# Attention, two-layer MoE and soft MoE on one core: leaky ReLU of H as one parametric ReLU on ScalarE

## The chip, the cores and the metric

The kernel runs on one core of a Trainium2 chip. The metric is the device time of one execution in microseconds (us); the times of before are the median of three runs. The engines are named as the profile names them: PE (TensorE matmuls) and PEld (its weight loads), DVE (VectorE), ACT (ScalarE), POOL (GpSimd), SP (the queue from which the DMAs are issued). Each works through its own list of instructions in order, and waits for another engine by semaphore.

## What is computed

Causal attention over 4 batches of 12 heads (448 positions, head size 64), then a two-layer MLP with a leaky ReLU, then a soft mixture of experts (32 slots, 8 experts):

```python
h = x @ w_in                    # x: 1792 x 768 (attention output), w_in: 768 x 2048
g = np.maximum(0.01 * h, h)     # leaky ReLU: the part that is changed
x = g @ w_out                   # w_out: 2048 x 768
logits = x @ phi                # soft MoE: softmax over tokens and over slots,
...                             # slot inputs, two expert layers, combination
```

## The kernel before

Attention runs in 24 steps, one for each pair of heads (six pairs to a batch). A step writes maxima of the scores (S), scores (T), their exponentials (P, ACT line 397), denominators (dn, rs) and the output O; line 472 scales O to x16, the two halves of x in 16 bits, from which the MLP reads.

H, the product x @ w_in, is made in units: for batch b and column block f (16 blocks of 128 columns) 18 matmuls add up H of 128 x 448 in one bank of PSUM. `up(b)` issues these units. While batch b+1 is in attention, `stage` mixes the sixteen units of batch b into it, about one unit to each of the 18 slots of a batch; this is so for batches 0, 1 and 2. In that time H has a single buffer (`HB[0]` is 1), so the next unit's first matmul waits until the last unit's H has been read. Batch 3's units come after attention, with three buffers, mixed with the transposes of earlier batches' g and the softmax sums (`combine`). After that only the experts are left, whose weights w stream in from memory.

Of each H, ACT line 628 makes g = H * iv, with a scale per partition, and DVE line 629 then reads H again and makes g = max(H * 0.01 iv, g). The two scales lie in iv, made by ACT lines 596 and 597 (one pair of 1-column instructions to a unit in batch 0, one pair of 16 columns for each later batch). H is free when both have read it. g of batches 0 and 1 is stored to memory (g_far, line 631, SP), and fetched back later (gb); g of batches 2 and 3 goes to the logits (L, line 578) and the transposes (gps, line 565).

Beside this, weights are prepared: w_in comes in as raw 64-bit numbers (raw_i), which DVE lines 199 to 201, ACT lines 196, 197 and 215 and POOL lines 216 and 223 turn into two 16-bit halves (w16); DVE lines 113 to 121 make the scale w_s for that. w_out (raw_o, cv_o) goes the same way to the small product wprime (tiles wt, wp_ps, wf_ps). Each new v (line 311) is reduced by DVE line 324.

The order on each engine is set by a scheduler that works with its own estimate of time; attention and `up` carry a higher priority than the preparation, and the matmuls issued through `in_order` keep the order in which they are written.

Of the kernel before, what the change touches and what calls it, by code (L numbers as in the profile page):

```python
# [10 lines left out]
F32 = mybir.dt.float32  # L11
# [4 lines left out]
AF = mybir.ActivationFunctionType  # L16
ALU = mybir.AluOpType
# [5 lines left out]
SLOPE = 0.01  # L23
# [11 lines left out]
def tile_attn_moe_softmoe(ctx: ExitStack, tc: tile.TileContext, q, k, v, w_in, w_out, phi, w1, w2, out, dbg=None):  # L35
    nc = tc.nc
# [11 lines left out]
    NF = DFF // 128  # L48
# [4 lines left out]
    const = ctx.enter_context(tc.tile_pool(name="const", bufs=1))  # L53
# [70 lines left out]
    inv_v = [None] * B  # L124
    inv_w = const.tile([128, NF], F32, name="inv_w")
    iv = [None] * B
# [153 lines left out]
    def need(u):  # L280
        while u not in ready:
            if not running:
                prep_start()
            prep_step()
# [276 lines left out]
    def transpose_g(b, f):  # L561
        g = gts[b, f]
        ps = ps_tr(f"gps{b}_{f}", (CP, NI, 128))
        for i in range(NI):
            tr(ps[:, i], g[:, CP * i : CP * (i + 1)], ident)
        dst = g_nat[:, :, 128 * f : 128 * (f + 1)]
        if f % 2 == 0:
            nc.scalar.copy(dst, ps)  # L568
        else:
            nc.vector.tensor_copy(dst, ps)  # L570

    def logits(b, f4):

        ps = ps_tr(f"L{b}_{f4}", (128, S))
        for f in range(f4, f4 + 4):
            r = 32 * (f % 4)
            need(("o", f))
            mm(ps[r : r + 32, :], wprime[:, f], gts[b, f], start=True, stop=True, skip_group_check=True)
        if f4 == 0:
            l4s[b] = mainp.tile([128, S], F32, tag="l4", name=f"l4_{b}")  # L580
            nc.vector.tensor_copy(l4s[b], ps)
        else:
            nc.vector.tensor_tensor(l4s[b], ps, l4s[b], ALU.add)

    def up(b, before=()):
        before = list(before)
        queue = []
        group = 0
        far = b < 2
        if b == B - 1:  # L590
            spare = xpool.tile([128, CHUNK // 4], F32, tag="x16", name="g_spare")
        iv[b] = const.tile([128, 2, NF], F32, tag="iv", bufs=2, name=f"iv{b}")

        def scales(j):

            nc.scalar.activation(iv[b][:, 0, j], inv_w[:, j], AF.Copy, scale=inv_v[b])
            nc.scalar.activation(iv[b][:, 1, j], iv[b][:, 0, j], AF.Copy, scale=SLOPE)

        if b > 0:
            scales(slice(0, NF))  # L600
        for f in range(NF):
            if b == 0:
                need(("i", f))
                scales(slice(f, f + 1))
            wq, fo = w16[f // 4], 128 * (f % 4)
            ps = psum.tile([128, S], F32, tag="H", bufs=HB[0], name=f"H{b}_{f}")
            step = 0
            for c in range(NP):
                for wh, xh in ((0, 0), (1, 0), (0, 1)):
                    mm(ps, wq[:, wh, c, fo : fo + 128], x16[b][:, c, xh, :], start=step == 0, stop=step == 17)  # L610
                    step += 1
                if b == B - 1:
                    if before:
                        before.pop(0)()
                    elif queue and queue[0] < f - (c < 3):
                        transpose_g(b, queue.pop(0))
                elif b == B - 2 and c in (2, 4) and queue and queue[0] < f - 1:
                    transpose_g(b, queue.pop(0))
            if not far and not before and f >= group + 5:
                logits(b, group)  # L620
                group += 4
            if b == B - 1 and f < NSPARE:
                g = spare[:, S * f : S * (f + 1)]
            else:
                g = mainp.tile([128, S], F32, tag="g", bufs=GBUF if b > 1 else 3, name=f"g{b}_{f}")
            gts[b, f] = g
            queue.append(f)
            nc.scalar.activation(g, ps, AF.Copy, scale=iv[b][:, 0, f : f + 1])  # L628
            nc.vector.scalar_tensor_tensor(g, ps, iv[b][:, 1, f : f + 1], g, ALU.mult, ALU.max)  # L629
            if far:  # L630
                nc.sync.dma_start(g_far[b, f], g)
            yield
        if far:
            return
        while before:
            before.pop(0)()
        while queue or group < NF:
            if group < NF:
                logits(b, group)
                group += 4  # L640
            for _ in range(4):
                if queue:
                    transpose_g(b, queue.pop(0))
# [119 lines left out]
    if True:  # L763
# [15 lines left out]
        for b in range(1, 4):  # L779
            if b == 3:  # L780
                tc_release(pools[1])
                tc_release(mainp)
                mainp = tc.alloc_tile_pool(name="mainp", bufs=1, reuse_waits="tile")
                pools[2] = tc.alloc_tile_pool(name="conv", bufs=1, side="right", reuse_waits="tile")
                load_raw()
                g_nat = mainp.tile([CP, NI, DFF], F32, name="g_nat")
            stage(SLOTS * NP, sum(EARLY[: b + 1]) if b < 3 else 2 * NF, up(b - 1))
# [54 lines left out]
        for _ in up(B - 1, spread(combine(B - 2)) + late):  # L842
            pass
# [127 lines left out]
        for x, (t0, nt, c0, cols) in enumerate(pieces):  # L971
# [4 lines left out]
            for h in (0, 1) if cols == DM else (c0 // DH,):  # L976
                for t in range(nt):
                    g = (t0 + t) % 4
# [55 lines left out]
```

## Time and profile before

| | |
|---|---|
| median of three runs | 726.96 us (726.59 to 730.62) |
| the profiled execution's own time | 722.34 us |
| its span, first to last instruction | 720.6 us |
| granted clock of TensorE, mean | 0.958 |
| PE busy | 615.5 us (85%) |
| DVE busy | 378.6 us (53%) |
| ACT busy | 304.7 us (42%) |
| POOL busy | 232.1 us (32%) |

The profiled execution lies 4.6 us under the median of the runs, and 1.7 us of its time lie outside the span. A share of the span is an average over stages. The first unit of H starts at 117 us, attention ends at about 480 us, batch 3's last unit at 594 us, and the experts take the rest.

### The profile page before, as it was taken

Reading aid. Unit: us, or ns where it says so; the run is one execution under the profiler, and the core shown is the slowest. Engines: PE = TensorE matmul, PEld = TensorE weight load, DVE = VectorE, ACT = ScalarE, POOL = GpSimd, SP = SyncE. Lnnn points to the kernel's source line nnn. Section 1 sums busy time; section 2 is a strip of 40 time slices with the busy share of each in tenths; the row PEclk is TensorE's granted clock in tenths of the full one; section 3 lists DMA queues with packets and bytes.
Section 4 is the critical chain, followed back from the end, with each engine's and each line's share of the span. In section 5 each row is a group of like instructions: output and inputs, shape, how many; then the busy total and the mean of one; then the engine's idle time right before and its main releaser. Section 6 shows DMA issues by size and latency. Waiting matters only on the chain.

```text
span 720.6 us, 12298 instructions
## 1 busy us (share of the span) xinstructions
PE 615.5 (85%) x4764; PEld 348.7 (48%) x4764; DVE 378.6 (53%) x941; ACT 304.7 (42%) x615; POOL 232.1 (32%) x247
## 2 busy tenths in 40 slices
PE   3788749888898999899999999999999998984572
PEld 2455535544454555455555555544655543541131
DVE  5887655688985654665475565444445333010022
ACT  1777643667875456554355544422222220110022
POOL 4477733467856423452143343310000000000000
PEclk9999977999999999999999999999999999999787
DMA  9933263455355446421153221018758148999988
GB/s 196 258 84 78 46 190 113 109 165 152 101 165 186 133 122 206 139 92 59 50 148 96 95 62 41 21 52 306 276 200 331 64 178 317 408 400 399 393 287 258
DMA packets 117706, 125.67 MB, mean 174 GB/s; under 512 B 69520, under 2 KB 99216, under 8 KB 117648
## 3 DMA queue, kind: packets, MB, share of 16 engines
q1 hardware_dynamic: 117648, 124.90, 53.6%
q8 instruction: 37, 0.61, 0.4%
q14 instruction: 21, 0.17, 0.1%
HBM read 105.74 MB, written 19.14 MB: 173 GB/s over the span
## 4 chain that ended last, share of the span: by engine, by line
PE 51%; DMA 14%; DVE 14%; ACT 9%; POOL 4%; issue 4%; SPq 2%; DVEq 0%; ACTq 0%; POOLq 0%
PE H L100 22%; DMA w<-in_moe_w_dram 8%; PE O L100 6%; PE gps L100 4%; DVE rs L439 3%; DMA v<-in_v_dram 3%; DVE junk L361 2%; DMA raw_o<-in_moe_w_out_dram 2%; PE pg L100 2%; PE ph L899 2%; PE T L100 2%; PE L L100 2%; ACT mr L373 2%; DMA raw_i_None<-in_moe_w_in_dram 2%; ACT g L628 2%
## 5 line engine op out<-in xcount | busy, mean ns | idle before, releaser
L100 PE MATMUL H<-x,w 128*128 128x448 f16 x1152 | 240.9, 354 | 7.3 <-DVE g L629 6.1
L100 PEld LDWEIGHTS <-w 128*128 128x128 f16 x1152 | 109.2, 98 | 109.9 <-issue 27.7
L361 DVE CUSTOM_DVE_ANT_0 junk<-S,mask 112x448 bf16<-112x448 f32 (+1 forms) x192 | 84.6, 441 | 37.5 <-PE S L100 35.3
L629 DVE SCALAR_TENSOR_TENSOR g<-H,iv,g 128x448 f32<-128x448 f32 x58 | 39.5, 682 | 75.5 <-ACT g L628 75.5
L401 POOL TENSOR_SCALAR_AFFINE_SELECT P<-P 112x448 f32<-112x448 f32 x48 | 29.4, 612 | 141.6 <-ACT P L397 141.5
L397 ACT ACTIVATE P<-T 112x672 f32<-112x672 f32 (+1 forms) x72 | 56.8, 790 | 23.1 <-PE T L100 22.9
L628 ACT ACTIVATE g<-H,iv 128x448 f32<-128x448 f32 x58 | 36.6, 631 | 70.5 <-PE H L100 62.3
L100 PE MATMUL T<-qkt 64*112 64x336 f32 (+3 forms) x576 | 59.2, 317 | 6.1 <-ACT P L397 5.4
L100 PE MATMUL O<-P,v 112*64 112x448 f32 (+3 forms) x384 | 56.9, 439 | 6.4 <-POOL P L401 6.0
L439 DVE RECIPROCAL rs<-rs 128x224 f32<-128x224 f32 x36 | 53.3, 1522 | 1.6 <-ACT rs L437 1.6
L100 PEld LDWEIGHTS T<-qkt 64*112 64x112 f32 x576 | 44.6, 182 | 14.4 <-ACT P L397 6.6
L979 PE MATMUL po<-w,hz 128*32 128x384 f32 x256 | 29.0, 575 | 25.2 <-DMA w<-in_moe_w_dram 25.2
L410 POOL TENSOR_TENSOR tsum<-tsum,P 112x448 f32<-112x448 f32 (+1 forms) x48 | 45.9, 956 | 2.8
L100 PEld LDWEIGHTS O<-P,v 112*64 112x64 f32 x384 | 26.8, 146 | 36.1 <-issue 17.3
L373 ACT ACTIVATE mr<-mps,own 128x112 fp32r<-128x112 f32 x96 | 26.2, 357 | 42.8 <-PE mps L100 42.8
L568 ACT COPY g_nat<-gps 112x512 f32<-112x512 f32 x32 | 18.7, 586 | 55.3 <-PE gps L100 55.3
L406 POOL TENSOR_TENSOR tsum<-P 112x672 f32<-112x672 f32 x24 | 40.7, 1698 | 1.8
L570 DVE COPY g_nat<-gps 112x512 f32<-112x512 f32 x32 | 22.1, 689 | 36.1 <-PE gps L100 35.8
L100 PE MATMUL S<-qkt 64*112 64x448 f32 (+1 forms) x192 | 33.0, 384 | 7.4 <-DVE mxe L361 5.7
L892 POOL MEMSET hz<- 128x256 f32 x2 | 0.6, 312 | 116.2 <-PE pg L100 116.2
L216 POOL TENSOR_TENSOR cv_i_None<-cv_i_None,cs_i_None 128x768 f32<-128x768 f32 x16 | 26.8, 1683 | 30.0 <-ACT cs_i_None L215 29.8
L100 PE MATMUL T<-mr,onesr 64*112 64x448 f32 (+1 forms) x192 | 32.1, 331 | 3.5 <-ACT mr L373 3.5
(184 smaller groups left out, 935.0 us busy)
## 6 DMA issues: line engine op xcount, KB each, us to landing
w<-in_moe_w_dram SPq DMA_DIRECT2D x32, 1536.0 KB, 18.2
raw_i_None<-in_moe_w_in_dram SPq DMA_DIRECT2D x16, 768.0 KB, 5.6
raw_o_None<-in_moe_w_out_dram SPq DMA_DIRECT2D x10, 768.0 KB, 5.0
g_far<-g SPq DMA_DIRECT2D x32, 224.0 KB, 2.0
gb<-g_far SPq DMA_DIRECT2D x8, 896.0 KB, 7.6
wo<-wsc SPq DMA_DIRECT2D x4, 1536.0 KB, 7.0
qk<-in_q_dram SPq DMA_DIRECT2D x48, 112.0 KB, 2.5
qk<-in_k_dram SPq DMA_DIRECT2D x48, 112.0 KB, 2.8
```

The source lines that it names most:

```text
L100: op(*args, **kwargs)
L216: nc.gpsimd.tensor_tensor(t, t, sg, ALU.mult)
L361: nc.vector.tensor_tensor_reduce(out=junk[:, :w], in0=ps[:, a, at : at + w], in1=mask[:, S - w :], scale=-1.0, scalar=3e38, op0=ALU.add, o ...
L373: nc.scalar.activation(mr[:, i], ps, AF.Copy, scale=own[:, i : i + 1])
L397: nc.scalar.activation(x[:, :, o : o + at], ps[:, :, :at], AF.Exp, scale=SCALE)
L401: nc.gpsimd.affine_select(out=d, in_=d, compare_op=ALU.is_ge, fill=0.0, base=0, pattern=[[0, 4], [1, CP]], channel_multiplier=-1,)
L406: nc.gpsimd.tensor_tensor(tsum[:CP], p[0][:CP, :, 0, CP:], p[0][:CP, :, 1, : S - CP], ALU.add)
L410: nc.gpsimd.tensor_tensor(y, y, p[1][:CP, :, j, : S - CP * (j + 2)], ALU.add)
L439: nc.vector.reciprocal(rs[:, c : c + S // 2], rs[:, c : c + S // 2])
L628: nc.scalar.activation(g, ps, AF.Copy, scale=iv[b][:, 0, f : f + 1])
L629: nc.vector.scalar_tensor_tensor(g, ps, iv[b][:, 1, f : f + 1], g, ALU.mult, ALU.max)
L979: nc.tensor.matmul(po[h][32 * g : 32 * g + 32], hp[:, (t0 + t) % 8], wt[:, t, DH * h - c0 : DH * (h + 1) - c0], start=t0 + t < 4, stop=t0 ...
```

## The change

One instruction takes the place of two: ACT makes g with its parametric ReLU function, scale iv and slope 0.01, straight from H. DVE line 629 goes, 64 times. The second half of iv and ACT line 597 go, 19 times. Everything behind line 625 moves up by two lines: the new line is 627, and g_far is stored by line 629.

```diff
-        iv[b] = const.tile([128, 2, NF], F32, tag="iv", bufs=2, name=f"iv{b}")
+        iv[b] = const.tile([128, NF], F32, tag="iv", bufs=2, name=f"iv{b}")
 
         def scales(j):
 
-            nc.scalar.activation(iv[b][:, 0, j], inv_w[:, j], AF.Copy, scale=inv_v[b])
-            nc.scalar.activation(iv[b][:, 1, j], iv[b][:, 0, j], AF.Copy, scale=SLOPE)
+            nc.scalar.activation(iv[b][:, j], inv_w[:, j], AF.Copy, scale=inv_v[b])
...
-            nc.scalar.activation(g, ps, AF.Copy, scale=iv[b][:, 0, f : f + 1])
-            nc.vector.scalar_tensor_tensor(g, ps, iv[b][:, 1, f : f + 1], g, ALU.mult, ALU.max)
+            nc.scalar.activation(g, ps, AF.Prelu, scale=iv[b][:, f : f + 1], alpha=SLOPE)
             if far:
                 nc.sync.dma_start(g_far[b, f], g)
```

The scheduler lays out the whole program anew. PE's list stays as it was but for four small neighbouring swaps. DVE's loses its 64 rows, and some preparation moves by a few places.

On DVE, behind the first two attention outputs of batch 1 (junk is the pass over the maxima, rs the inverse denominators, cv_i raw w_in), before:

```order
L439 RECIPROCAL rs_1680<-rs_1680 128x224 x2
L199 TENSOR_REDUCE w_am_1837<-cv_i_None 128x1
L472 SCALAR_TENSOR_TENSOR rs_1680<-O_1603,v_s,rs_1680 128x448
L629 SCALAR_TENSOR_TENSOR g_4_1730<-H_4_1711,iv_1378,g_4_1730 128x448
L200 TENSOR_SCALAR cv_i_None<-cv_i_None 128x768
L361 ISA junk_1_0_1771,mxe_144<-S_1_1768,mask 112x224
```

and of the change:

```order
L439 RECIPROCAL rs_1672<-rs_1672 128x224 x2
L199 TENSOR_REDUCE w_am_1825<-cv_i_None 128x1
L472 SCALAR_TENSOR_TENSOR rs_1672<-O_1597,v_s,rs_1672 128x448
L200 TENSOR_SCALAR cv_i_None<-cv_i_None 128x768
L361 ISA junk_1_0_1761,mxe_144<-S_1_1758,mask 112x224
```

Only g_4 is gone; the rest stands in the same order.

On SP, at units 9 to 11 of batch 0, before:

```order
L302 DMA qk_2267<-in_q_dram 112x4x64 x2
L631 DMA g_far<-g_9_2203 128x448
L302 DMA qk_2267<-in_k_dram 112x4x64 x2
L173 DMA raw_o_None<-in_moe_w_out_dram 128x1536 x2
L311 DMA v_2516<-in_v_dram 112x8x64
L631 DMA g_far<-g_10_2296 128x448
L631 DMA g_far<-g_11_2364 128x448
```

and of the change:

```order
L629 DMA g_far<-g_9_2184 128x448
L302 DMA qk_2247<-in_q_dram 112x4x64 x2
L302 DMA qk_2247<-in_k_dram 112x4x64 x2
L173 DMA raw_o_None<-in_moe_w_out_dram 128x1536
L629 DMA g_far<-g_10_2275 128x448
L311 DMA v_2490<-in_v_dram 112x8x64
L173 DMA raw_o_None<-in_moe_w_out_dram 128x1536
L629 DMA g_far<-g_11_2341 128x448
```

The store of g_10 now stands ahead of the next load of v, and one load of raw_o behind it. The same happens to two more loads of v, at g_2 and g_13.

On ACT, the whole program of the change holds one table load, ahead of its first copy, as before:

```order
L1027 UNCONDITIONAL_BRANCH
L338 ACT_TABLE_LOAD
L338 CAST qkt_187<-qkps_0_188 128x448
L338 CAST qkt_187<-qkps_1_195 128x448
```

## Rows read from the trace of the kernel before

**Rows 1.** Busy time of each engine by stage (x instructions), granted clock, DMA share, GB/s

```profile
117.00:240.00 123.00, 110.54 (x759) 61.35 (x756) 94.19 (x237) 79.68 (x150) 74.40 (x59) 0.99 0.48 140
240.00:362.00 122.00, 116.07 (x895) 68.57 (x895) 69.53 (x155) 60.90 (x130) 44.06 (x41) 0.99 0.35 109
362.00:480.00 118.00, 111.48 (x833) 65.10 (x831) 62.67 (x142) 56.49 (x125) 41.01 (x45) 0.99 0.27 79
480.00:594.00 114.00, 112.34 (x754) 61.40 (x752) 51.26 (x102) 28.75 (x55) 1.03 (x1) 1.00 0.59 212
594.00:721.00 127.00, 82.86 (x835) 37.00 (x834) 21.14 (x64) 14.75 (x35) 2.62 (x16) 0.87 0.94 351
```

**Rows 2.** PE's waits, whole span: total us, times, longest

```profile
PE H L100 <- DVE g L629: 6.1, 6, 1.6
...
PE H L100 <- DVE w_s L118: 1.2, 1, 1.2
...
PE L L100 <- DVE g L629: 1.1, 2, 0.6
```

**Rows 3.** Groups by line, whole span: busy us, mean ns, idle before

```profile
L628 ACT ACTIVATE g<-H,iv 128x448 f32<-128x448 f32 x58 | 36.6, 631 | 70.5 <-PE H L100 62.3 <-PE L L100 6.6 <-DMA raw_o_None<-in_moe_w_out_dram 1.6
...
L629 DVE SCALAR_TENSOR_TENSOR g<-H,iv,g 128x448 f32<-128x448 f32 x58 | 39.5, 682 | 75.5 <-ACT g L628 75.5
...
L597 ACT ACTIVATE iv<-iv 128x1 f32<-128x1 f32 (+1 forms) x19 | 3.7, 201 | 0.2
...
L690 ACT ACTIVATE et<-lt,nm 128x448 f32<-128x448 f32 x4 | 2.5, 636 | 12.5 <-PE pl L100 12.5
...
L338 ACT ACT_TABLE_LOAD x1 | 1.3, 1283 | 0.8 <-PEq L1018 0.8
```

**Rows 4.** Timeline at three waits of H: start us, length us, engine and line

```profile
144.99 0.69 DVE L629 SCALAR_TENSOR_TENSOR g<-H,iv,g 128x448 f32<-128x448 f32 x1 [1.10 <-ACT g L628]
145.73 3.56 PE L100 MATMUL H<-x,w 128*128 128x448 f16 x18 [1.55 <-DVE g L629]
...
189.41 0.64 ACT L628 ACTIVATE g<-H,iv 128x448 f32<-128x448 f32 x1
191.57 0.67 DVE L629 SCALAR_TENSOR_TENSOR g<-H,iv,g 128x448 f32<-128x448 f32 x1
192.30 5.18 PE L100 MATMUL H<-x,w 128*128 128x448 f16 x18 [1.21 <-DVE w_s L118]
...
228.45 3.56 PE L100 MATMUL H<-x,w 128*128 128x448 f16 x18 [1.46 <-DVE g L629]
```

**Rows 5.** PE's waits for DVE's other work in 117:240, 240:362 and 362:480

```profile
PE S L100 <- DVE mxe L361: 2.3, 3, 1.1
...
PE w_ps L111 <- DVE qkt L339: 0.9, 1, 0.9
...
PE wf_ps L100 <- DVE qkt L339: 2.0, 1, 2.0
...
PE wf_ps L100 <- DVE qkt L339: 1.1, 1, 1.1
```

**Rows 6.** The chain that ended last: its shares; first and last DVE g in it

```profile
PE H L100 22%; DMA w<-in_moe_w_dram 8%; PE O L100 6%; PE gps L100 4%; DVE rs L439 3%; DMA v<-in_v_dram 3%; DVE junk L361 2%; DMA raw_o<-in_moe_w_out_dram 2%; PE pg L100 2%; PE ph L899 2%; PE T L100 2%; PE L L100 2%; ACT mr L373 2%; DMA raw_i_None<-in_moe_w_in_dram 2%; ACT g L628 2%
...
151.44 0.69 DVE g L629
...
591.80 0.69 DVE g L629
```

**Rows 7.** SP's timeline where v is moved behind a store of g

```profile
199.75 0.38 SPq L311 DMA_DIRECT2D v<-in_v_dram  x1
200.22 6.64 SPq L631 DMA_DIRECT2D g_far<-g  x2
```

**Rows 8.** Stretches of 4 us around the wait at 192 us, columns as in rows 1

```profile
188.00:192.00 4.00, 2.17 (x26) 1.76 (x27) 4.00 (x10) 3.64 (x7) 3.92 (x5) 1.00 0.22 90
192.00:196.00 4.00, 3.70 (x12) 1.48 (x12) 4.00 (x7) 1.46 (x4) 3.68 (x4) 0.57 0.69 172
```

## The prediction

> **What bounds the kernel now.** I read the stages first. From 117 to 594 us, where all 64 units of H lie, PE is busy 110.5 of 123, 116.1 of 122, 111.5 of 118 and 112.3 of 114 us [rows 1]. PE is the bound, and all that any edit of other engines can give there is PE's idle time: 12.5 + 5.9 + 6.5 + 1.7 = 26.6 us, nearly half of it in the first stretch. There DVE is the next busiest, 94.2 of 123 us [rows 1]. From 594 us on the experts' weights load at a DMA share of 0.94 [rows 1]; those loads start as PE frees buffers, so that stage moves with the end of H and its own length stays.
>
> Then I asked who ends PE's waits. Six waits of H for DVE's pass over g total 6.1 us, and two of the logits L 1.1 us [rows 2]. One more, 1.2 us, is put down to DVE's w_s [rows 2], but the timeline shows DVE's g ending at 191.57 + 0.67 = 192.24, just ahead of H at 192.30 [rows 4]: it is the same wait. So 8.4 us of PE's idle time ends with the instruction that the change removes.
>
> The third view is the chain that ended last. Line 629 is in it in 10 pieces, the first and last of which are [rows 6]; they add up to 5.7 us. So the views give two sizes, a wait sum and a chain sum.
>
> **The change part by part.** *DVE's pass goes.* It is 58 instructions of 682 ns plus six of the same shape on g's spare tile [rows 3], 64 x 0.68 = 43.6 us of DVE. Most of it lies beside PE's work and gives nothing. What it gives on the path comes in two kinds.
>
> First, H (single-buffered) and L are released when ACT ends, not DVE. Of the 8.4 us I take each wait as far as ACT's end allows. At 145.73 DVE began at 144.99, straight behind ACT, while PE had waited 1.55 us [rows 4]: with H released at ACT's end, the wait shrinks by about 0.73 us, and 0.8 stays. The same holds for the 1.46 us wait at 228.45 [rows 4], which keeps 0.7. At 192.30 ACT had ended at 189.41 + 0.64 = 190.05 and g sat in DVE's queue [rows 4], so all of the 1.21 goes; the other waits are short or of this sort. 8.4 - 0.8 - 0.7 = 6.9 us.
>
> Second, DVE reaches what stood behind g 0.68 us sooner. Five waits of PE for other DVE work come at the end of a run of DVE instructions with a g in it: two of the three waits of S for mxe, one of w_ps and two of wf_ps [rows 5]. Each can shrink by at most 0.68 us: 5 x 0.68 = 3.4 us. Sum of both kinds: 10.3 us.
>
> *ACT's pass stays one pass.* The parametric ReLU does not occur in the trace of before. The nearest rows are ACT's scaled copy of the same tile, 631 ns, and an Exp of the same shape with one per-partition operand, 636 ns [rows 3]: two functions, one price. From below, the price could be some 0.1 us lower and from above 0.1 us higher if the operands are read in another way; the chain holds ACT's g for 2% of the span [rows 6], 14 us or some 22 executions, so that is 2.2 us either way. I take no difference and keep 2.2 us for the range.
>
> *Line 597 goes*, 19 x 0.20 = 3.7 us of ACT [rows 3]. I cost it at nothing: it runs beside PE, in stretches where ACT has idle time (79.7 busy of 123 us [rows 1]). Without that cover it would give up to 3.7 us.
>
> *Order.* DVE and PE keep their sequence. On SP three loads of v now stand behind a store of g that they were ahead of. At one of them the load was issued 0.47 us before the store [rows 7]; without DVE's pass the store is ready earlier, so a load loses half a microsecond at most, three of them 1.5 us. Behind v waits DVE's reduction and whatever stands behind it on DVE; transfers of v hold 3% of the chain [rows 6]. They hold more than nothing and less than all of it: I take a third, 0.5 us.
>
> *Sum.* Not all 10.3 us arrive: where PE gets ahead it meets the next producer earlier, and waits there instead. The chain's 5.7 us count only what ended last and nothing that follows. I take the middle of both, 8.0 us, less 0.5 us for v: **7.5 us**. Against the profiled execution's own 722.34 us this is 714.8; that execution lies 4.6 us under the median of the runs, so for the median it is 726.96 - 7.5 = **719.5 us**, 1.0% less. A measurement of this kernel can tell 0.5%, 3.6 us, from no change.
>
> [...] In the trace, the ACT pass takes 631 ns and the DVE pass 682 ns on the same f32 tile from PSUM [rows 3]. [...]
>
> **The rivals.**
>
> *The gain is larger.* [...] Chance 0.16.
>
> *The time is hidden anyway.* In the first stretch ACT and POOL are busy 79.7 and 74.4 of 123 us too [rows 1], and transfers of v have 3% of the chain [rows 6]. If PE, freed of one wait, runs into ACT's cs, POOL's w or v's landing each time, only the waits at the end of batch 3 (1.1 us of L [rows 2]) and about another microsecond are kept: a gain of 2 us, 725 us. Chance 0.22.
>
> *Parametric ReLU is dearer, and ACT becomes the wait.* If the function with its second slope cost more per element, each unit's release of H would come later. With 22 executions in the chain [rows 6], the point at which the 7.5 us are spent is 7.5 / 22 = 0.34 us, a pass of 0.97 us. A pass twice as long, 1.26 us, costs 22 x 0.63 = 13.9 us and gives 726.96 - 7.5 + 13.9 = 733 us. Against it speak the equal 631 and 636 ns of the two functions in rows 3. Chance 0.06.
>
> *The function does not share a table with Exp.* [...] The program of the change has one table load in all, as the part on the change shows, so this hardly remains. [...] Chance 0.02.
>
> **How the numbers follow.** The forecast, a gain of 4 to 11 us, has the remaining 0.54. The range's low end is the larger gain with the pass 2.2 us cheaper on the path, 713.5 - 2.2, about 711.5 us; its high end is the hidden case, to 725.5. Outside lie the two dear cases (0.08), and the part of the hidden case in which next to nothing is left (about 0.1). Faster by over 0.5%: nearly all of the forecast (0.52), the larger gain (0.16) and a few hundredths of the hidden case, 0.71. Within 0.5%: the rest of the hidden case and the forecast's edge, 0.21. Slower: 0.08.
>
> **What the profile after should show.** ACT's g at about 631 ns, 64 times, and one table load; DVE's busy time down from the 378.6 us of the table by about 43.6 us to some 335; no wait of H for DVE, and waits of H for ACT's g of 0.7 to 0.8 us where 145.73 and 228.45 stood. PE's busy time unchanged but for the clock, its idle time from 117 to 594 us down from 26.6 to about 19 us, most of it in batch 0's sixteen units; the last stage still about 127 us long. The prediction is wrong if ACT's g is over 0.7 us, if PE's waits reappear in full on ACT's mr, POOL's P or v's transfer, if the experts' stage grows by what the earlier stages lose, or if clock falls appear in new places.

## The result, and the profile after

The changed kernel takes 718.52 us (median of 4 runs, 715.01 to 719.55) against 726.78 us for the kernel before (median of 4, 726.18 to 730.62): a ratio of 0.988, with an interval of 0.984 to 0.992. A second comparison with more runs, told below, gave 0.9924 [0.9891, 0.9958]. The means are 725.62 us before (105 executions of the experiments, standard error 0.27, without six that lie over 1.5% above the fastest, with which the mean would be 0.3 us higher) and 720.07 us after (16, standard error 0.72, none left out): **5.5 us less, 0.8%**. The forecast was a gain of 7.5 us, to 719.5 us, in a range of 711.5 to 725.5.

The profiled execution of the change took 718.55 us with a span of 716.8 us; the one of before had 720.6 us. This pair alone shows 3.8 us. The profiled execution of before was a good one, 722.34 us where its mean is 725.62, so single spans are compared below only where several kernels agree.

The first part of the page of the change:

```profile
PE 616.6 (86%) x4764; PEld 350.0 (49%) x4764; DVE 338.9 (47%) x877; ACT 302.8 (42%) x596; POOL 231.5 (32%) x247
```

The groups by line of the change, columns as in [rows 3]:

```profile
L627 ACT ACTIVATE g<-H,iv 128x448 f32<-128x448 f32 x58 | 36.6, 631 | 71.9 <-PE H L100 63.8 <-PE L L100 6.5 <-DMA raw_o_None<-in_moe_w_out_dram 1.6
```

The parametric ReLU costs ACT 631 ns, as the scaled copy did [rows 3]. That price was as forecast. DVE's 58 + 6 passes are gone; DVE is busy 338.9 us where some 335 were expected, so its other instructions took some 3.9 us longer together. The stages, columns as in [rows 1]:

```profile
117.00:240.00 123.00, 110.76 (x765) 61.99 (x762) 86.48 (x222) 79.00 (x141) 74.01 (x59) 0.99 0.47 142
240.00:362.00 122.00, 116.42 (x891) 68.93 (x890) 59.09 (x138) 60.00 (x128) 43.71 (x40) 0.97 0.35 108
362.00:480.00 118.00, 111.37 (x837) 65.54 (x837) 53.87 (x129) 56.85 (x124) 41.17 (x45) 0.99 0.27 79
480.00:594.00 114.00, 113.72 (x765) 62.24 (x761) 40.53 (x86) 29.11 (x57) 1.04 (x1) 1.00 0.60 215
594.00:721.00 127.00, 80.42 (x829) 34.82 (x828) 20.19 (x62) 14.80 (x35) 2.60 (x16) 0.86 0.93 348
```

PE's idle time from 117 to 594 us is 12.2 + 5.6 + 6.6 + 0.3 = 24.7 us. It was 26.6 us [rows 1], and 19 were expected. The stage in which PE idles most, the first, still idles 12.2 of its 123 us. PE's waits of the change over the whole span (us in total, times, longest) tell why:

```profile
PE T L100 <- ACT mr L373: 6.3, 13, 2.0
...
PE S L100 <- ACT P L397: 2.2, 1, 2.2
...
PE H L100 <- ACT g L627: 1.5, 3, 0.6
```

Two of these in the kernel before:

```profile
PE T L100 <- ACT mr L373: 3.5, 13, 0.9
...
PE S L100 <- ACT P L397: 0.9, 1, 0.9
```

No wait of H or L ends with DVE any more, where 8.4 us did [rows 2, 4]. Three waits of H remain, for ACT's g, 1.5 us together. But the waits of T for ACT's mr have grown from 3.5 us to 6.3, those of S for P from 0.9 to 2.2. PE's timeline of the change shows where (start us, length us, and in brackets the idle time before it and what ended it):

```profile
145.00 3.56 PE L100 MATMUL H<-x,w 128*128 128x448 f16 x18 [0.59 <-ACT g L627]
151.23 3.56 PE L100 MATMUL H<-x,w 128*128 128x448 f16 x18 [0.65 <-ACT g L627]
...
174.60 0.60 PE L111 MATMUL w_ps<-ident,w_am 128*128 128x128 f32 x2 [2.90 <-DVE qkt L339]
...
199.90 0.46 PE L100 MATMUL T<-mr,onesr 64*112 64x448 f32 x2 [1.79 <-ACT mr L373]
...
213.12 0.36 PE L100 MATMUL S<-qkt 64*112 64x224 f32 x2 [2.24 <-ACT P L397]
...
223.07 0.45 PE L100 MATMUL T<-mr,onesr 64*112 64x448 f32 x2 [1.97 <-ACT mr L373]
```

The third of these instructions in the kernel before:

```profile
176.00 0.49 PE L111 MATMUL w_ps<-ident,w_am 128*128 128x128 f32 x2 [0.86 <-DVE qkt L339]
```

The wait of 1.55 us at 145.73 [rows 4] is now 0.59 us, in the place that the prediction gave and near its 0.8; the one at 228.45, which was to keep 0.7, is gone. The second row was a wait of 0.86 us before, at 152.17, which the prediction counted as gone whole; 0.65 us of it stay. The four long waits below it are ended by attention's chain of producers (qkt, mr, P). At the first of them PE arrives 3.4 us earlier than before (174.60 - 2.90 = 171.70 against 176.00 - 0.86 = 175.14) but goes on only 1.4 us earlier, so it stands 2 us longer.

### The profile page after: what moved, and what is told of

It is laid out like the page before. It is cut to its first block, busy times and chain, and to the rows that moved or that the text cites. A ratio compares the mean times of both kernels' runs of the same rounds, so it can differ in the third digit from the quotient of the medians.

```text
span 716.8 us, 12198 instructions
## 1 busy us (share of the span) xinstructions
PE 616.6 (86%) x4764; PEld 350.0 (49%) x4764; DVE 338.9 (47%) x877; ACT 302.8 (42%) x596; POOL 231.5 (32%) x247
## 4 chain that ended last, share of the span: by engine, by line
PE 55%; DMA 14%; DVE 12%; ACT 8%; POOL 3%; issue 3%; SPq 2%; DVEq 0%; ACTq 0%
PE H L100 24%; DMA w<-in_moe_w_dram 8%; PE O L100 6%; PE gps L100 4%; PE T L100 3%; DVE rs L439 2%; PE ph L897 2%; DMA v<-in_v_dram 2%; PE L L100 2%; PE pg L100 2%; DVE junk L361 2%; DMA raw_i_None<-in_moe_w_in_dram 2%; ACT mr L373 2%; PE qkps L100 2%; DMA raw_o<-in_moe_w_out_dram 2%
## 5 line engine op out<-in xcount | busy, mean ns | idle before, releaser
L439 DVE RECIPROCAL rs<-rs 128x224 f32<-128x224 f32 x36 | 53.3, 1521 | 12.6 <-ACT rs L437 12.6
L100 PEld LDWEIGHTS O<-P,v 112*64 112x64 f32 x384 | 27.5, 150 | 34.8 <-issue 16.5
L339 DVE TENSOR_TENSOR qkt<-qkps,qkt 128x448 fp32r<-128x448 f32 x48 | 28.1, 618 | 14.0 <-ACT qkt L338 14.0
```

What stands on the lines that cost most here:

```text
L100: op(*args, **kwargs)
L339: nc.vector.tensor_tensor(st[:, j, 1], p, st[:, j, 0].bitcast(F32), ALU.subtract)
L439: nc.vector.reciprocal(rs[:, c : c + S // 2], rs[:, c : c + S // 2])
```

## The experiments

**How firm a difference is.** Both kernels were run again unedited, the change as this:

> The changed kernel once more, unedited, to narrow the ratio and to have a second profile. The forecast was a gain of 7.5 us (ratio 0.990); the first four runs gave 0.988. In the first pair of profiled executions the spans differ by 3.8 us only (720.6 and 716.8). Theory A (the relief of DVE and of H's release): ratio 0.986 to 0.992 again, and the sixteen units of batch 0 finish 3 to 5 us sooner than in the profile of before when no fall of the clock lies among them. Theory B (the difference is mostly where the clock happens to fall): single runs scatter by 4 us and more around a ratio nearer to 0.995.

It took 720.5 us (median of 12), ratio 0.9924 [0.9891, 0.9958]. The kernel before against itself:

> The kernel before, unedited, as a second profile and as a measure of the noise: ratio 0.997 to 1.003. Over the runs so far a mean granted clock lower by 0.01 went with 4 to 5 us more, in both kernels; the profile of before that the forecast was made from has 0.958, the highest of its kernel but one, and its time is 4 us under the mean. A profile at a clock near 0.950 should show more falls of the clock between 117 and 590 us than the three of the first, and batch 0 longer than 121.4 us.

727.31 us, ratio 1.0015 [0.998, 1.005]. So the change is faster by 0.4 to 1.1%, and executions of one kernel scatter by some 3 us around their mean.

The second profile of before was of more use than its time. PE's waits in it from 117 to 250 us:

```profile
PE H L100 <- DVE g L629: 7.2, 5, 2.6
PE S L100 <- DVE mxe L361: 3.5, 2, 2.6
PE T L100 <- ACT mr L373: 1.3, 3, 0.9
PE H L100 <- DVE w_s L118: 1.2, 1, 1.2
PE O L100 <- POOL P L401: 1.1, 1, 1.1
PE S L100 <- ACT P L397: 0.9, 1, 0.9
PE w_ps L111 <- DVE qkt L339: 0.9, 1, 0.9
PE mps L100 <- DVE mxe L361: 0.3, 1, 0.3
PE w_ps L111 <- DVE w_m L113: 0.2, 1, 0.2
```

They add up to 16.6 us, 13.3 of them ended by DVE; in the profile on which the prediction was made it was 12.6 and 9.2. The table sums this view for every profile of the study; the kernels below the second row are told further down. "Batch 0" is the time from ACT's g of unit 0 to that of unit 16, and "idle" the part of it in which PE is not busy.

| kernel | for DVE | for ACT | for POOL | sum, us | batch 0, us | idle, us |
|---|---|---|---|---|---|---|
| before | 9.2 | 2.3 | 1.1 | 12.6 | 121.4 | 12.5 |
| before, again | 13.3 | 2.2 | 1.1 | 16.6 | 128.4 | 16.5 |
| old form in batch 0 alone | 12.3 | 2.2 | 1.1 | 15.6 | 127.5 | 15.6 |
| new form in the last unit alone | 11.9 | 2.4 | 1.0 | 15.3 | 128.9 | 15.2 |
| after | 4.2 | 7.8 | 0 | 12.0 | 120.7 | 12.2 |
| after, again | 4.2 | 8.1 | 0 | 12.3 | 125.7 | 12.3 |
| new form in batch 0 alone | 4.2 | 8.4 | 0 | 12.6 | 124.2 | 12.4 |
| new form in all but the last unit | 4.2 | 8.6 | 0 | 12.8 | 124.3 | 12.6 |
| after + reduction on DVE | 4.4 | 5.8 | 2.5 | 12.7 | 119.6 | 12.5 |
| after + second pass on ACT | 1.5 | 9.3 | 0.9 | 11.7 | 121.9 | 11.5 |
| after + release by DVE | 10.8 | 1.8 | 0 | 12.6 | 125.6 | 12.5 |
| after + pass over g on DVE | 7.6 | 6.0 | 0 | 13.6 | 128.4 | 13.8 |
| after, scaling of cs on DVE | 4.2 | 3.5 | 0 | 7.7 | 118.3 | 7.9 |
| after, cast of w on DVE | 15.1 | 1.6 | 0 | 16.7 | 130.4 | 16.5 |

In the first four rows batch 0 has the old form, in the next four the new one with nothing added. From the first four to the next the waits for DVE fall from 11.7 to 4.2 us on average, those for ACT rise from 2.3 to 8.2, and sum and idle time fall from 15.0 to 12.4. The profile from which the prediction was read is the exception: PE idled there in batch 0 hardly longer than in the change. Over all four stages from 117 to 594 us the second profiles have 29.6 us of idle time before and 24.2 after; the mean of two falls from 28.1 to 24.5, by 3.6 us. A part of the rest may lie at the end: from ACT's last g to the last instruction it takes 129.5 and 128.5 us in the two profiles of before, 126.4 and 127.1 in those of the change. The runs with the last unit, below, bear on that.

**Is it DVE's time?** The change with a reduction of g put on DVE, whose result nobody reads, gives DVE nearly all of its work back and leaves H's release with ACT (idle_t is a tile of one column):

```diff
             nc.scalar.activation(g, ps, AF.Prelu, scale=iv[b][:, f : f + 1], alpha=SLOPE)
+            nc.vector.tensor_reduce(idle_t, g, AX.X, ALU.max)
```

> The changed kernel with one more DVE instruction behind each g: a maximum over the columns of g into a column that nobody reads (a reduction of 512 columns takes 0.685 us in the trace of before, so some 0.6 us for these 448, 64 times, 39 us). H is released by ACT, and g's readers wait for ACT alone; only DVE's time comes back. Theory A1 (DVE's freed time is the gain): most of it is lost, 724 to 726 us, ratio 0.997 to 1.000. Theory A2 (the release of H and of g is the gain): it stays, 720 to 721.5 us, ratio 0.992 to 0.994.

716.42 us (median of 6), ratio 0.9888 [0.9845, 0.9931]. The group by line shows that the load was there:

```profile
L629 DVE TENSOR_REDUCE idle_t<-g 128x1 f32<-128x448 f32 x58 | 35.8, 617 | 73.3 <-ACT g L628 73.3
```

58 passes of 617 ns and six more on the spare tile are 39.5 us, where the change had removed 43.6, and the whole gain stays. DVE's time, and that DVE reaches its next instruction 0.68 us sooner, is not what the change gives.

**Is it ACT's time, or how soon H comes free after it?** The change with ACT's pass made twice:

```diff
             nc.scalar.activation(g, ps, AF.Prelu, scale=iv[b][:, f : f + 1], alpha=SLOPE)
+            nc.scalar.activation(g, ps, AF.Prelu, scale=iv[b][:, f : f + 1], alpha=SLOPE)
```

> The parametric ReLU of each H is made twice by ACT, the second over the first: 64 more passes of 0.63 us on ACT, 40 us, and H is released 0.63 us later. By the forecast's rival of a dear function, 22 executions of g in the chain cost 22 x 0.63 = 13.9 us over the changed kernel: ratio to before about 1.007. If ACT has room (42% busy) and H's release by ACT is rarely waited for, it costs 3 to 5 us: ratio 0.994.

720.38 us, ratio 0.992 [0.9886, 0.9953]: nothing is lost. The groups by line, and below them PE's waits from 117 to 250 us:

```profile
L628 ACT ACTIVATE g<-H,iv 128x448 f32<-128x448 f32 x58 | 36.9, 637 | 0.7
...
L627 ACT ACTIVATE g<-H,iv 128x448 f32<-128x448 f32 x58 | 36.6, 631 | 79.6 <-PE H L100 72.3 <-PE L L100 7.3
```

```profile
PE H L100 <- ACT g L628: 6.4, 4, 2.3
PE T L100 <- ACT mr L373: 2.9, 4, 1.6
PE S L100 <- DVE mxe L361: 1.5, 3, 0.6
PE O L100 <- POOL P L401: 0.9, 1, 0.9
```

H comes free 0.64 us later, nearly as late as behind a DVE pass that starts at once, and PE waits 6.4 us for it, about as much as it once waited for DVE. But where it waits for H it has less to wait for mr, P and mxe afterwards, and the sum, 11.7 us, is about that of the change. A wait of H was not worth its length. The run speaks on line 597 too: ACT carries some 40 us more at no loss, so the 3.7 us that it was spared there can hardly be part of the gain.

**H's release through DVE's queue.** The change with a DVE instruction of one column that reads H, so that the tile is free only when DVE comes to it:

```diff
             nc.scalar.activation(g, ps, AF.Prelu, scale=iv[b][:, f : f + 1], alpha=SLOPE)
+            nc.vector.scalar_tensor_tensor(idle_t, ps[:, :1], SLOPE, g[:, :1], ALU.mult, ALU.max)
```

> ACT makes g by parametric ReLU; DVE then reads one column of H and of g into a tile that nobody reads (about 0.2 us, 64 times). DVE keeps 13 us of the 43.6 us, and H is released through DVE's queue as in the kernel before, behind ACT; g's readers no longer wait for DVE. If the release of H is what counts, 2 to 3 us of the gain are left, ratio 0.996; if DVE's freed time is what counts, 4 to 6 us are left, ratio 0.992 to 0.994.

722.37 us, ratio 0.9953 [0.9921, 0.9984]; the mean is 723.04 us, 3.0 above that of the change (standard error 0.9), and 2.2 above its second set of runs, made beside it (standard error 1.0). The group by line:

```profile
L629 DVE SCALAR_TENSOR_TENSOR idle_t<-H,g 128x1 f32<-128x1 f32 x58 | 9.0, 155 | 77.9 <-ACT g L628 77.8
```

PE's waits in it from 117 to 250 us:

```profile
PE S L101 <- DVE mxe L362: 5.0, 2, 3.9
PE H L101 <- DVE idle_t L629: 3.1, 4, 1.4
PE w_ps L112 <- DVE qkt L340: 2.7, 1, 2.7
PE T L101 <- ACT mr L374: 1.8, 4, 1.0
```

This instruction takes 155 ns against 617 of the reduction, and the kernel is slower than the one with the reduction. What sets the two edits apart is that the short one holds H. So 2 to 3 of the 5.5 us are put down to H waiting in DVE's queue no more, behind mxe, qkt or w_s. The times show this and the waits do not: the sum is 12.6 us, PE idles 24.0 us from the first g to the last where the change has 24.5 and 24.2, and only 3.1 us of its waits are for H. Where in the program the loss lies is open. That the length of the pass that ends the wait matters little is shown for ACT alone, by the doubled pass; the other half of the gain, between this kernel and the one before, can still hold DVE's longer pass on H, which no run separates.

**g through DVE's queue as well.** The change with a pass of DVE over g in place that leaves its values as they are:

```diff
             nc.scalar.activation(g, ps, AF.Prelu, scale=iv[b][:, f : f + 1], alpha=SLOPE)
+            nc.vector.scalar_tensor_tensor(g, g, 1.0, g, ALU.mult, ALU.max)
```

> ACT makes g by parametric ReLU, and DVE then makes a pass over g in place that changes nothing (max of 1.0 g and g), so DVE has its 64 passes of about 0.68 us again and g's readers wait for them, but H is released by ACT alone. If the release of H is what the change gains (6.9 us of the 10.3 in the forecast's sum), this keeps 4 to 6 us of the gain: ratio 0.992 to 0.995. If DVE's freed time is what counts, it is within 2 us of before, ratio 0.997 to 1.003.

732.33 us, ratio 1.0091 [1.0054, 1.0128], slower than before. It is no clean test: its passes were not those of before. The instructions of its line (durations in ns: shortest, median, longest):

```profile
L628 DVE SCALAR_TENSOR_TENSOR g<-g x58: 610/626/4032, 121.4 to 603.1; 128x448 f32<-128x448 f32 x58
```

Before's passes, with H from PSUM, lay between 666 and 686 ns without exception. The timeline of DVE's pass and of POOL's instructions around two of the long ones (start us, length us):

```profile
157.74 0.61 DVE L628 SCALAR_TENSOR_TENSOR g<-g 128x448 f32<-128x448 f32 x1
...
182.98 3.26 POOL L216 TENSOR_TENSOR cv_i_None<-cv_i_None,cs_i_None 128x768 f32<-128x768 f32 x2 [6.10 <-ACT cs_i_None L215]
184.65 2.06 DVE L628 SCALAR_TENSOR_TENSOR g<-g 128x448 f32<-128x448 f32 x1 [0.93 <-ACT g L627]
186.19 2.03 POOL L223 TENSOR_TENSOR w<-cv_i_None,w 128x768 f16<-128x768 f32 x1
...
215.37 2.32 POOL L406 TENSOR_TENSOR tsum<-P 112x672 f32<-112x672 f32 x1
216.27 4.03 DVE L628 SCALAR_TENSOR_TENSOR g<-g 128x448 f32<-128x448 f32 x1
217.66 1.63 POOL L232 TENSOR_TENSOR cv_o_None<-cv_o_None,cs_o_None 128x768 f32<-128x768 f32 x1
219.25 0.57 POOL L401 TENSOR_SCALAR_AFFINE_SELECT P<-P 112x448 f32<-112x448 f32 x1
219.80 2.01 POOL L216 TENSOR_TENSOR cv_i_None<-cv_i_None,cs_i_None 128x768 f32<-128x768 f32 x1
```

The pass at 184.65 begins inside POOL's pair, which runs to 186.24, and ends at 186.71, 0.47 us later; POOL's next instruction then takes 2.03 us instead of 1.64. The one at 216.27 ends at 220.30, 0.48 us behind the third of POOL's in a row. The one at 157.74, where POOL stands still, takes 0.61 us. So it is with all eleven of the 17 passes up to 250 us that took over 640 ns: each began inside an instruction of POOL and ended 0.47 to 0.49 us behind one. The other six began where POOL stood still and took 0.61 to 0.63 us. The eleven took 11.7 us more than the median of 626 ns would give. In the kernel before, 24 of the 64 passes with H from PSUM began inside an instruction of POOL too, and took 0.67 to 0.69 us as the others did. How much of the slowdown comes from g standing in the queue, and how much from these long passes, stays open.

**Which batches?** The kernel before with the new form in batch 0 alone, and with `b > 0` as the condition in all but batch 0 (the second column of iv stays where the old form reads it):

```diff
-            nc.scalar.activation(g, ps, AF.Copy, scale=iv[b][:, 0, f : f + 1])
-            nc.vector.scalar_tensor_tensor(g, ps, iv[b][:, 1, f : f + 1], g, ALU.mult, ALU.max)
+            if b == 0:
+                nc.scalar.activation(g, ps, AF.Prelu, scale=iv[b][:, 0, f : f + 1], alpha=SLOPE)
+            else:
+                nc.scalar.activation(g, ps, AF.Copy, scale=iv[b][:, 0, f : f + 1])
+                nc.vector.scalar_tensor_tensor(g, ps, iv[b][:, 1, f : f + 1], g, ALU.mult, ALU.max)
```

> The change for batch 0's sixteen units alone; the other 48 keep ACT's copy and DVE's pass. The forecast put 7 of the 10.3 us of its sum into batch 0, where DVE is busiest (94.2 of 123 us). By it 65 to 75% of the gain is kept, 3.5 to 4 of the 5 to 6 us: ratio 0.994 to 0.996. If the gain is spread by the number of units, a quarter is kept: ratio 0.998.

> The reverse: batch 0 keeps the two passes, the other 48 units have the parametric ReLU. By the forecast a quarter to a third of the gain: ratio 0.997 to 0.998. If it is spread by the number of units, three quarters: ratio 0.994 to 0.995.

724.32 us, ratio 0.9975 [0.9946, 1.0004], and 723.05 us, 0.9974 [0.9941, 1.0006]. Neither is clear of no change by itself. By the means they are 1.5 and 2.7 us under the kernel before, with a standard error of 0.7 each. They don't bear out that most of the gain lies in batch 0: by the ratios it is half of the two together, by the means about a third, and neither share is firm. The profiles don't decide it either. Batch 0 took 121.4, 128.4, 128.9 and 127.5 us in the four with the old form there, mean 126.6, and 120.7, 125.7, 119.6, 124.2 and 124.3 us in five with the new form, mean 122.9: 3.7 us, with a standard error of about 2. Of this, 2.6 us are idle time of PE; the rest scatters with the granted clock of the stretch, 0.95 to 0.99 in the four and 0.95 to 1.00 in the five. Batch 3 took 97.4 or 97.5 us in every one.

**The end of batch 3.** In before's profile PE waits 0.56 us for L there, and the run of matmuls pg behind it has 5.34 us, at a granted clock of 0.50 from 599 to 601 us, against 3.64 us in that of the change, all at 1.00. This fall of the clock seemed to go with the wait, some 2.2 us at one place. Before and the change:

```profile
597.59 5.34 PE L100 MATMUL pg<-g_nat,dn 112*32 112x512 f32 x32 [0.38 <-DVE dn L703]
```

```profile
596.09 3.64 PE L100 MATMUL pg<-g_nat,dn 112*32 112x512 f32 x32 [0.38 <-DVE dn L701]
```

Two kernels tested it, the edit as above with two other conditions for the new form, the last unit alone and all units but the last:

```diff
+            if (b, f) == (B - 1, NF - 1):
```

> The kernel before with the change at one unit of 64 alone, the last of batch 3. In five profiles so far in which a DVE or second ACT pass stands behind the last H, the way from ACT's last g to the end of pg lasts 11.0 to 11.8 us in four, with pg at 5.2 to 5.4 us, and in the four where ACT's g is the last word it lasts 9.4 us, with pg at 3.69 us and no fall of the clock. Theory A3 (a good part of the gain is this end: the pass itself, and a fall of the clock behind it): this one unit gains 2 to 2.5 us of the 5 to 6, ratio 0.9965, and pg takes 3.69 us. By the forecast's sum this unit is worth 0.6 us: ratio 0.999.

```diff
+            if (b, f) != (B - 1, NF - 1):
```

> The reverse: the parametric ReLU at every unit but the last of batch 3. Theory A3: 2 to 2.5 us of the gain are lost, ratio 0.9955 to 0.996, and pg takes 5.2 to 5.4 us again. By the forecast's sum it stays at 0.992 to 0.993.

725.81 us, ratio 0.999 [0.9963, 1.0016], and 720.32 us, ratio 0.9916 [0.9885, 0.9946]. PE's timeline with the new form in the last unit alone, and then in all but the last:

```profile
596.47 1.73 PE L100 MATMUL L<-g,wprime 128*32 128x448 f32 x8
...
602.30 5.34 PE L100 MATMUL pg<-g_nat,dn 112*32 112x512 f32 x32 [0.38 <-DVE dn L706]
```

```profile
590.48 0.94 PE L100 MATMUL L<-g,wprime 128*32 128x448 f32 x2 [0.62 <-DVE g L633]
...
595.47 5.34 PE L100 MATMUL pg<-g_nat,dn 112*32 112x512 f32 x32 [0.38 <-DVE dn L707]
```

Without the wait pg has its 5.34 us all the same, so the fall doesn't need it. Nor does the wait always bring it: over the 14 profiles pg takes 5.1 to 5.3 us in five of six with a wait of L behind the last unit, and in four of eight without one. From ACT's last g to the end it takes 128.7 us on average in the six and 127.2 in the eight. The times show less: by the means the last unit alone gives 0.5 us (standard error 0.9), and the kernel that leaves it out is 0.1 us above the change (standard error 1.2). What the end is worth is therefore between nothing and some 2 us.

**Taking the next waits away.** The waits that came up are ended by ACT, whose queue also scales and casts weights in batch 0. Two steps were moved to DVE, which now has room: the scaling of cs, and the cast of w.

```diff
-        nc.scalar.activation(sg, sg, AF.Copy, scale=s_w)
+        nc.vector.tensor_scalar(sg, sg, s_w, None, ALU.mult)
```

> The changed kernel with the scaling of w_in's signs (line 215, 16 passes of 0.93 us) moved from ACT to DVE, which makes the scale just before. In the changed kernel PE's waits in batch 0 have gone over from DVE (9 to 13 us before, 4 us after) to ACT (2 us before, 8 us after), chiefly to ACT's mr and P. If ACT's queue is what PE waits for there, this gains 2 to 4 us more: 716 to 718 us, ratio 0.987 to 0.990. If those waits only stand where others would, nothing: ratio 0.992.

```diff
-            nc.scalar.copy(hi, w)
+            nc.vector.tensor_copy(hi, w)
```

> The changed kernel with the 16-bit upper half of w_in (line 222, 14 passes of 0.83 us) moved from ACT to DVE. As for the signs: 2 to 3 us more if ACT's queue is the wait of batch 0, ratio 0.988 to 0.990; but in the run with a DVE pass over g in place, DVE passes that touch SBUF alone took up to 4 us, so it may cost as much: ratio 0.992 to 0.996.

The first took 722.91 us, ratio 0.9934 [0.9903, 0.9965], mean 720.91: the waits of the table fall to 7.7 us in its profile, batch 0 to 118.3 us, but the time is that of the change. The second took 730.55 us, ratio 1.0078 [1.0041, 1.0114]. The instructions of its line, in ns, and then the timeline of one cast with POOL's pair:

```profile
L222 DVE CAST w<-cv_i_None x14: 553/1095/1991, 45.1 to 228.5; 128x768 f16<-128x768 f32 x14
```

```profile
146.50 3.26 POOL L216 TENSOR_TENSOR cv_i_None<-cv_i_None,cs_i_None 128x768 f32<-128x768 f32 x2 [5.77 <-ACT cs_i_None L215]
148.18 1.99 DVE L222 CAST w<-cv_i_None 128x768 f16<-128x768 f32 x1 [1.50 <-POOL cv_i_None L216]
```

The cast begins inside POOL's pair and ends at 150.17, 0.41 us behind the pair's end at 149.76, much as the pass over g does. PE's waits for DVE from 117 to 250 us rise to 15.1 us. No kernel of the study is clearly faster than the change.

## Why the prediction was right

Direction and size came out: 5.5 us by the means and 8.3 by the first medians, where 7.5 was forecast. Step by step:

- *ACT's pass keeps its price.* Right: 631 ns, one table load of 1283 ns in the profile, as before. The 0.1 us by which the price might have lain higher or lower was the author's estimate, and no run shows it. The price mattered less than the prediction thought: a doubled pass costs nothing that can be measured, where the rival of the dear function put 13.9 us on it. That rival's step "22 executions in the chain, so 22 times the difference" was wrong. A chain of one execution shows what ended last there; lengthen one link here and PE waits less at the next.
- *H and L are released when ACT ends: 6.9 us.* The place is right, the price and its reading are not. Waits of H and L for DVE went from 8.4 us to none, with 1.5 us left for ACT. But the sizing by ACT's end, 0.7 us a wait, falls: H comes free 0.64 us later in the kernel with two passes on ACT without loss. What the kernel with the one-column instruction shows is that H's way through DVE's queue costs 2 to 3 us; that it is the standing behind other work there is the likely reading, and not shown by its waits.
- *DVE reaches other work 0.68 us sooner: 3.4 us.* Wrong. With nearly all of DVE's load put back the gain stays.
- *Not all of it arrives; the middle of wait sum and chain sum, 8.0 us.* The reason is right: in batch 0, 7.5 us of waits for DVE go and 5.9 come back under ACT's name, which is near the sign "reappear in full" by which the prediction was to be wrong. The size is in part luck. One term of the sum was worth nothing and the other less than half of its price, and taking the middle made up for most of that. PE's idle time, expected to fall from 26.6 us to 19, was 24.7; by two profiles of each kernel it fell by 3.6 us. The last stage, which the prediction left at its length, may have given up to 2 us.
- *Most of it in batch 0.* Not borne out: half by the ratios, a third by the means, with intervals too wide for a firm share.
- *Line 597, v's loads, the end of batch 3.* Putting line 597 at nothing fits the doubled pass on ACT. Batch 3 kept its length to 0.1 us, and the last unit gave no time that can be told from none. The half microsecond for v was not tried by itself.
- *The range's low end, 711.5 us.* The 713.5 us in it are 726.96 less 10.3 us and two falls of the clock of 1.6 us each. No run shows that such falls go with the waits for DVE. In stretches of 4 us from 117 to 593 us the granted clock was under 0.95 at three places in the profile of before and at three in that of the change: the one behind 192 us (0.57 [rows 8]) is gone, and one of 0.73 came at 173 us.

Open remain the split between batch 0 and the rest, what makes up the half of the gain that the one-column instruction does not take back, and what g's own way through DVE's queue costs without the long passes beside POOL. The kernel with the extra reduction came out 3.3 us under the change by the means, in six runs (standard error 1.4); their mean granted clock was 0.956 against 0.951, which by the rate given below goes with some 2 us.

## What to carry to other kernels

Where a wait ends with an instruction, ask also what stood in front of that instruction in its queue: a DVE instruction of 155 ns that held H cost 2 to 3 us here, and one of 617 ns that released nothing cost none. Count as gain only what is left once the next producers have been met: of 7.5 us of waits that vanished, nearly 6 returned under another name. And before a single profile's sum is priced, compare it with a second profile of the same kernel: here the same view of the same kernel gave 9.2 and 13.3 us.

## What the runs showed of the hardware beside

DVE's pass over g in place took 610 to 4032 ns, and the cast of w moved to DVE 553 to 1991 ns; the eleven long passes over g up to 250 us each began inside an instruction of POOL. The pass that reads H from PSUM stayed at 666 to 686 ns beside POOL too, and the reduction of g lay at 604 to 622 ns in all 58. Reading g in place of H so made the pass dearer here: 1.31 us on average for the 17 up to 250 us, against 0.68.

Executions of one kernel scatter with TensorE's clock as granted on average: within the kernels of the study, 0.01 less of the mean granted clock goes with 3.7 us more time. Before and after had the same mean, 0.951, so the gain is not a matter of runs that drew a better clock. The profile of before had 0.958 and lay 3.3 us under its mean; the first profile of the change had 0.946, and lay 1.5 us under its own all the same.
